# A long convolution beside a gated MLP on one Trainium2 core: the second token tile fetched by transfers of its own, and a new issue order

## The chip, the cores and the metric

The kernel runs on one core of a Trainium2 chip. The time is the device time of one launch in microseconds (us), and less is better. The median of three runs is 256.29 us (256.15 to 256.86).

The engines are named as the profile names them: PE (TensorE, matmuls; PEld is its weight load), DVE (VectorE), ACT (ScalarE), POOL (GpSimd) and SP (SyncE). SP does no arithmetic here. It issues nearly all transfers between DRAM and the on-chip memory, one after another, and so does ACT for a few at the start. Each engine works through its own list of instructions in order.

## What is computed

There are 2048 tokens of 640 channels. With `xn` the layer norm of `A_q`, the result is `A_q` plus a gated long convolution plus a gated MLP (cut to what matters):

```python
def _A_ref(q, k, v, shift_k, ssm_k, ssm_D):
    k_shift = ...            # four taps over time, by channel
    kv = k_shift * v
    y = ...                  # kv convolved with ssm_k over 2048 steps, by FFT of 4096
    y = y + kv * ssm_D
    return q * y
def _B_ref(x, w_gate, w_up, w_down):
    g = x @ w_gate           # 640 -> 1728
    u = x @ w_up
    return (sigmoid(g) * u) @ w_down
xn = _layernorm(A_q)
return A_q + _A_ref(xn, A_k, A_v, A_shift_k, A_ssm_k, A_ssm_D) + _B_ref(xn, B_w_gate, B_w_up, B_w_down)
```

## The kernel before

**Tokens.** The tokens stand in 16 tiles of 128, tile `m` in `acc[:, m, :]`, which holds `A_q` at first and collects both branches. A tile is fetched by quarters of 32 partitions (`load_x`, whose transfer is recorded at profile line L352): quarters 0 and 1 through SP's queue, 2 and 3 through ACT's for tiles 0 to 3, all through SP's for the others. Tiles 0 to 3 make up pass 0, tiles 4 to 7 pass 1, and so on to pass 3.

**The MLP.** For each pass the tokens are normed (statistics L639 to L659, norm L683 on DVE or L685 on ACT) and transposed, on PE for passes 0 and 1 (L705, copied to `xnT` at L314 or L315) and by a transposing transfer through DRAM for passes 2 and 3 (L699). Then 14 chunks of the hidden width follow: five matmuls for the gate and five for the up side (L770, output in `g`), sigmoid on ACT (L735, L729), product on DVE (L737, L732) into `hT`. Pass 0 begins with two chunks in pieces of 128 tokens (L750), so that the first product needs only tile 0. After the chunks, seven matmuls at a time (L786) multiply `hT` with `wd`, and DVE adds the result to `acc` (L798).

Weights are fetched in pieces `w{pass}_{n}`, even `n` for the gate and odd for the up side (`load_w`, L368 to L378). Passes 0 and 1 share one set; passes 2 and 3 load theirs again. Four buffers called `w` hold most pieces, and a further four, `wv`, lie in the buffer `V` until the convolution needs it. A piece that is to go into a buffer in use waits for the buffer's last matmul.

**The convolution.** It runs over ten groups of channels. DVE forms `kv` from `kt` and `vt` (L470 to L488); PE transforms over one factor of the time axis (L508, 32 short matmuls; copied to `T`), then the other (L528, 32 short matmuls each; copied to `S`); DVE multiplies the spectra (L552 to L567), for groups 3 to 9 after two transfers that swap the halves of `S` (L548, `P<-S`); PE transforms back (L580, and L582 for group 0; copied to `V`) and, once for each half of the channels, last L612, 64 short matmuls at a time, whose result is multiplied by the normed tokens (L620) and added to `acc` (L621). The results of L508, L528, L580 and L612 go through three PSUM buffers called `c`, those of L705, L770 and L786 through two called `g`.

**Order.** The function first records every operation with what it reads and writes and on which engine it may run (`plan.op`). An operation is a group of instructions: one transfer, five matmuls, one copy. `ORDER` is a list, written out in full, of the numbers of all operations, which count the calls of `plan.op`. `emit` goes through it and issues each operation on its engine; so it sets the order on each engine, and also which of several buffers an operation gets: an empty one, else the one whose user finished longest ago. Copies that may run on either ACT or DVE run on ACT, unless their number is in `ON_DVE`.

**The start.** Operation 4 is a group of 12 matmuls on zeros, the later seven of the same kind are operation 104 (L816). Operations 5 to 8 fetch tile 0, 10 to 13 tiles 1 to 3 together (120 KB a quarter), 14 and 16 the first halves of the first two weight pieces, operation 9 is a square root on ACT of no further use (L821).

The lines around the end: the result leaves through `store` (L630), four quarters for each range of tiles, the last tile in two halves of 320 columns.

Of the kernel before, what the change touches and what calls it, by code (L numbers as in the profile page):

```python
# [15 lines left out]
ACT = mybir.ActivationFunctionType  # L16
# [26 lines left out]
def _dft_tables():  # L43
# [34 lines left out]


ORDER = [  # L80
    2, 0, 5, 4, 6, 8, 7, 10, 71, 72, 12, 73, 1, 11, 13, 14, 42, 74, 75, 91, 96, 76, 77, 78, 16, 81, 86, 79, 80, 92,
    625, 87, 97, 88, 104, 82, 83, 98, 84, 85, 93, 99, 626, 89, 90, 94, 148, 100, 18, 149, 102, 61, 607, 62, 9, 643,
    608, 63, 101, 150, 103, 19, 639, 645, 153, 641, 43, 627, 629, 152, 640, 642, 635, 67, 637, 628, 630, 17, 609, 611,
    64, 636, 15, 68, 638, 617, 619, 610, 44, 20, 650, 154, 612, 66, 651, 618, 652, 151, 157, 65, 620, 158, 155, 156,
    613, 3, 615, 621, 57, 58, 614, 105, 623, 107, 622, 616, 644, 106, 624, 603, 605, 631, 56, 119, 604, 633, 108, 632,
    606, 115, 599, 116, 634, 646, 601, 600, 648, 109, 647, 111, 122, 60, 59, 602, 112, 661, 113, 649, 673, 662, 665,
    674, 677, 110, 114, 24, 120, 663, 22, 675, 29, 664, 666, 676, 45, 32, 26, 23, 25, 133, 679, 117, 678, 121, 118,
    123, 130, 653, 680, 654, 27, 134, 21, 681, 31, 135, 683, 655, 682, 28, 181, 124, 183, 136, 656, 669, 684, 657,
    658, 670, 30, 33, 672, 34, 126, 35, 667, 163, 659, 668, 660, 162, 165, 127, 685, 671, 164, 125, 716, 36, 167, 166,
    687, 718, 686, 37, 168, 38, 743, 182, 688, 47, 744, 159, 172, 745, 171, 717, 703, 161, 719, 720, 705, 50, 725,  # L90
    727, 169, 39, 170, 704, 160, 51, 706, 726, 173, 128, 178, 698, 728, 729, 174, 180, 700, 707, 131, 175, 699, 709,
    708, 54, 186, 176, 701, 710, 177, 179, 721, 739, 192, 298, 711, 702, 723, 129, 184, 741, 740, 53, 40, 95, 194,
    299, 722, 41, 52, 195, 185, 742, 193, 187, 724, 188, 189, 69, 196, 227, 218, 228, 201, 300, 46, 689, 48, 691, 734,
    690, 49, 190, 199, 736, 233, 202, 692, 197, 200, 301, 234, 198, 55, 217, 191, 693, 137, 304, 730, 735, 216, 737,
    229, 132, 732, 213, 219, 215, 230, 731, 733, 712, 738, 714, 221, 694, 138, 696, 203, 713, 205, 214, 207, 695, 715,
    831, 139, 697, 231, 220, 209, 303, 143, 204, 232, 206, 747, 224, 222, 210, 811, 140, 141, 761, 208, 305, 223, 748,
    211, 762, 751, 225, 235, 237, 236, 833, 226, 263, 212, 764, 772, 254, 264, 755, 265, 144, 269, 302, 252, 253, 267,
    771, 239, 266, 255, 268, 756, 758, 749, 270, 285, 750, 256, 287, 257, 142, 306, 752, 759, 249, 251, 286, 238, 241,
    250, 242, 753, 70, 258, 832, 760, 240, 763, 754, 757, 746, 260, 262, 288, 407, 245, 773, 146, 291, 775, 246, 243,
    765, 244, 271, 272, 786, 788, 247, 766, 261, 273, 410, 275, 767, 318, 248, 274, 259, 768, 320, 769, 319, 277, 278,  # L100
    289, 770, 290, 409, 276, 321, 324, 325, 279, 294, 322, 323, 787, 292, 297, 789, 774, 293, 315, 317, 280, 776, 316,
    782, 307, 784, 326, 281, 783, 790, 282, 308, 310, 327, 838, 283, 785, 839, 309, 284, 777, 311, 840, 295, 340, 354,
    779, 328, 312, 812, 342, 341, 330, 834, 778, 358, 411, 355, 780, 329, 331, 296, 356, 313, 360, 781, 334, 335, 826,
    145, 791, 836, 357, 332, 835, 828, 333, 414, 345, 361, 837, 338, 827, 359, 314, 829, 336, 412, 817, 337, 344, 830,
    822, 362, 343, 351, 819, 339, 824, 823, 352, 818, 363, 792, 346, 825, 347, 408, 353, 793, 404, 427, 348, 364, 349,
    365, 795, 413, 820, 797, 794, 350, 428, 431, 796, 406, 405, 432, 821, 367, 370, 799, 433, 429, 430, 383, 802, 798,
    424, 366, 368, 804, 434, 371, 369, 425, 417, 803, 374, 800, 372, 147, 375, 373, 805, 416, 813, 435, 801, 806, 419,
    384, 418, 421, 420, 422, 385, 454, 808, 807, 815, 426, 386, 809, 387, 376, 814, 377, 436, 415, 463, 464, 378, 379,
    438, 437, 866, 844, 449, 388, 816, 450, 886, 389, 453, 854, 810, 451, 845, 469, 465, 380, 467, 439, 855, 926, 423,
    927, 847, 390, 381, 470, 468, 850, 460, 466, 441, 858, 440, 443, 444, 860, 462, 851, 452, 841, 382, 861, 853, 461,  # L110
    391, 392, 393, 455, 842, 867, 864, 928, 442, 457, 485, 490, 397, 394, 456, 471, 843, 846, 862, 486, 398, 399, 401,
    458, 487, 400, 863, 445, 446, 868, 489, 459, 447, 865, 848, 870, 488, 448, 499, 500, 472, 877, 503, 501, 879, 505,
    849, 504, 474, 878, 476, 506, 473, 475, 502, 491, 496, 479, 498, 480, 477, 478, 497, 852, 493, 507, 492, 494, 856,
    483, 481, 484, 880, 508, 495, 857, 869, 859, 482, 510, 521, 871, 571, 512, 515, 516, 527, 522, 523, 881, 509, 872,
    883, 531, 533, 511, 528, 578, 532, 529, 874, 534, 882, 513, 514, 884, 585, 530, 535, 873, 875, 519, 520, 524, 525,
    536, 876, 929, 931, 885, 517, 930, 887, 518, 901, 526, 592, 932, 549, 888, 903, 538, 906, 550, 551, 553, 537, 539,
    541, 540, 555, 902, 890, 552, 889, 556, 904, 542, 554, 543, 544, 891, 905, 892, 557, 897, 894, 899, 893, 898, 558,
    395, 396, 545, 895, 921, 896, 907, 546, 900, 923, 908, 922, 910, 559, 924, 912, 547, 548, 560, 561, 563, 564, 562,
    565, 913, 566, 569, 567, 915, 909, 568, 570, 579, 911, 925, 580, 914, 933, 582, 917, 572, 916, 934, 581, 583, 935,
    919, 584, 573, 918, 575, 574, 576, 586, 920, 944, 577, 960, 938, 587, 939, 589, 945, 402, 593, 941, 588, 590, 591,  # L120
    966, 962, 594, 947, 936, 963, 596, 942, 937, 943, 595, 961, 597, 965, 598, 940, 946, 403, 970, 969, 948, 950, 949,
    952, 968, 951, 953, 954, 971, 956, 973, 967, 975, 974, 972, 955, 964, 957, 958, 977, 979, 978, 976, 959, 981, 983,
    982, 980
]
ON_DVE = [
    101, 103, 133, 134, 135, 136, 656, 658, 884, 875, 525, 518, 915, 570, 581, 575
]


# [90 lines left out]
def kernel(  # L220
# [100 lines left out]
    def dma(fn, nd, run, q="SP", **kw):  # L321
        few = 1.4 if nd <= 64 and run > 1000 else 1.0
        plan.op({q: (0.48 + nd / 8000.0, lambda: fn(nc.sync if q == "SP" else nc.scalar))},
                size=1.05 * few * nd * (10.6 + run / 23.8) / 16e3 + 0.03, **kw)
# [26 lines left out]
    def load_x(q, m0, m1, eng, pri):  # L351
        dma(lambda e: e.dma_start(acc[32 * q:32 * q + 32, m0:m1, :], xq4[q][:, m0:m1, :]), 32, 1280 * (m1 - m0), q=eng,  # L352
            w=[("acc", m, q) for m in range(m0, m1)], pri=pri)
# [8 lines left out]
    def load_w(tr, n, pri):  # L362
        key, w = weight(tr, n)
        nb = max(0.0, pri - 14)
        kw = dict(pri=pri, nb=nb)
        al = [(key[0], "V")] if key == ("wv", 0) else [] if len(key) == 2 else [(key[0], "w")]
        if n == 6:
            dma(lambda e: e.dma_start(w()[:, :, 0:192], wgr[:, :, 1536:1728]), 640, 384, w=[key + (0,)], alloc=al, **kw)  # L368
            dma(lambda e: e.dma_start(w()[:, :, 256:384], wur[:, :, 1536:1664]), 640, 256, w=[key + (1,)], **kw)
            dma(lambda e: e.dma_start(w()[:, :, 192:256], wur[:, :, 1664:1728]), 640, 128, w=[key + (2,)], **kw)  # L370
            return
        f0, src = 512 * (n // 2), (wgr, wur)[n % 2]
        if tr == 0 and n < 2:
            for h in range(2):
                dma(lambda e, h=h: e.dma_start(w()[:, :, 256 * h:256 * h + 256], src[:, :, f0 + 256 * h:f0 + 256 * h + 256]),
                    640, 512, w=[key + (h,)], alloc=al if h == 0 else (), pri=pri + 0.5 * h)
        else:
            dma(lambda e: e.dma_start(w()[:], src[:, :, f0:f0 + 512]), 640, 1024, w=[key + (0,), key + (1,)], alloc=al, **kw)  # L378
# [425 lines left out]
    FIX = -1e6  # L804
# [14 lines left out]
        load_x(q, 0, 1, "SP", FIX)  # L819
        load_x(q + 2, 0, 1, "ACT", FIX)  # L820
    plan.op({"ACT": (1.35, lambda: nc.scalar.activation(eps2, eps, ACT.Sqrt))}, r=[("eps",)], w=[("eps2",)], pri=FIX + 2)  # L821
    for q in range(2):
        load_x(q, 1, 4, "SP", FIX + 1)
        load_x(q + 2, 1, 4, "ACT", FIX + 1)
    load_w(0, 0, FIX + 2)
    load_w(0, 1, FIX + 2)
    dma(lambda e: e.dma_start(Ft[:], Fdram.ap()), 128, 640, w=[("F",)], pri=11.0, nb=9.0)
# [100 lines left out]
```

## Time and profile before

| | |
|---|---|
| median of three runs | 256.29 us |
| the profiled execution | 259.03 us |
| its span | 257.1 us |
| mean granted clock of PE, as a share | 0.989 |
| moved by transfers | 41.44 MB, mean 161 GB/s |

The span of the profile runs from the first instruction to the last transfer; the profiled execution's own time has some 1.9 us around it, and the executions without a profile are shorter by 2.7 us. In the lines that follow, a timeline line gives the start in us, the duration, the engine (SPq and ACTq are issues of transfers), the source line, the operation with its output and input, and in brackets how long the engine had been idle before it and what ended that. "issue" there means that nothing which the profile shows was waited for. Lines of the windows give a stretch, then its length and for each engine the busy time and the instructions, then the granted clock of PE, the share of the 16 transfer engines that was busy, and GB/s.

### The profile page before, as it was taken

How to read it: one execution, taken by the hardware profiler on the slowest of the kernel's cores; microseconds unless marked ns; L12 is line 12 of the kernel's file. 1: busy time of each engine (PE TensorE's matmuls, PEld its weight loads, DVE VectorE, ACT ScalarE, POOL GpSimd, SP SyncE). 2: the span in 40 equal slices, each digit the busy share in tenths (PEclk: the TensorE clock that was granted, in tenths of full speed). 3: DMA queues.
4: the chain of work that ended last, by engine and by line, in shares of the span. 5: the costliest groups of instructions: out<-in, count | busy, mean ns of one | idle time of the engine just before them, and what ended most of it. 6: DMA issues, size and time to landing. Idle time of an engine off the chain costs nothing.

```text
span 257.1 us, 9461 instructions
## 1 busy us (share of the span) xinstructions
PE 242.6 (94%) x4231; PEld 146.0 (57%) x4231; DVE 201.1 (78%) x337; ACT 175.3 (68%) x259; POOL 0.7 (0%) x6
## 2 busy tenths in 40 slices
PE   8999999999998999999999997699999999798991
PEld 3744446764454567666554544477765554365770
DVE  4613624679999799999999999669999998786731
ACT  3722789577998899787998885655788785452200
POOL 1000000000000000000000000000000000000000
PEclk9999999999999999999999999989999999999998
DMA  6999999999994527999999829953217386002472
GB/s 179 303 289 226 214 304 130 154 143 180 223 261 123 136 87 223 157 135 131 162 185 262 227 44 301 208 128 87 54 32 207 69 273 177 10 3 56 105 188 70
DMA packets 91024, 41.44 MB, mean 161 GB/s; under 512 B 66656, under 2 KB 88104, under 8 KB 90664
## 3 DMA queue, kind: packets, MB, share of 16 engines
q1 hardware_dynamic: 90792, 40.52, 74.3%
q8 instruction: 33, 0.54, 0.9%
q10 hardware_dynamic: 192, 0.33, 0.4%
q14 instruction: 7, 0.06, 0.1%
HBM read 30.61 MB, written 5.24 MB: 139 GB/s over the span
## 4 chain that ended last, share of the span: by engine, by line
PE 79%; DVE 7%; ACT 5%; DMA 4%; issue 3%; ACTq 1%; DVEq 0%
PE g L770 36%; PE g L786 25%; PE c L528 7%; PE c L612 4%; PE c L580 3%; DMA w<-in_B_w_up_dram 2%; PE c L508 2%; ACT S L314 1%; DMA acc<-in_A_q_dram 1%; DVE kvt L488 1%; PE c L750 1%; PE g L705 1%; ACT T L317 1%; DVE hT L737 1%; DVE ta L475 1%
## 5 line engine op out<-in xcount | busy, mean ns | idle before, releaser
L770 PE MATMUL g<-xnT,w 128*128 128x512 bf16 x380 | 90.9, 379 | 1.7 <-DMA w<-in_B_w_up_dram 1.4
L786 PE MATMUL g<-wd,hT 128*128 128x320 bf16 x448 | 67.3, 303 | 2.9 <-issue 2.9
L770 PEld LDWEIGHTS <-w 128*128 128x128 bf16 x380 | 34.9, 98 | 39.8 <-DMA w<-in_B_w_up_dram 1.9
L786 PEld LDWEIGHTS <-hT 128*128 128x128 bf16 x448 | 42.3, 99 | 19.7 <-issue 3.1
L314 ACT CAST S<-c 128x1024 bf16<-128x1024 f32 x40 | 39.6, 1022 | 8.5 <-PE c L528 8.3
L737 DVE TENSOR_TENSOR hT<-sig,g 128x512 bf16<-128x512 bf16 x32 | 21.9, 685 | 17.6 <-PE g L770 17.3
L770 PE MATMUL g<-xnT,V 128*128 128x512 bf16 x140 | 32.6, 379 | 0.0
L735 ACT ACTIVATE sig<-g 128x512 bf16<-128x512 f32 x32 | 19.2, 600 | 15.2 <-PE g L770 13.6
L798 DVE TENSOR_TENSOR acc<-g,acc 128x320 bf16<-128x320 f32 x32 | 15.5, 488 | 17.0 <-PE g L786 16.8
L528 PEld LDWEIGHTS <-Mt 64*128 64x128 f16 x1280 | 20.4, 96 | 9.2 <-issue 8.6
L528 PE MATMUL c<-T,Mt 64*128 64x64 bf16 x1280 | 23.1, 192 | 2.7 <-issue 2.7
L317 ACT ACTIVATE T<-c 128x1024 bf16<-128x1024 f32 x20 | 19.9, 1027 | 5.2 <-PE c L508 5.0
L770 PEld LDWEIGHTS <-V 128*128 128x128 bf16 x140 | 13.4, 98 | 15.4 <-issue 0.4
L488 DVE TENSOR_TENSOR kvt<-ta,vt 128x1024 bf16<-128x1024 bf16 x10 | 21.4, 2142 | 0.1
L314 ACT CAST V<-c 128x1024 bf16<-128x1024 f32 x18 | 18.2, 1025 | 3.2 <-PE c L580 3.1
L314 ACT CAST T<-c 128x1024 bf16<-128x1024 f32 x19 | 18.8, 1023 | 1.6 <-PE c L508 1.6
L729 ACT ACTIVATE sig<-g 128x512 bf16<-128x512 f32 x18 | 10.8, 600 | 5.2 <-PE g L770 4.2
L561 DVE TENSOR_TENSOR S<-S 128x1024 bf16<-128x1024 bf16 x20 | 13.8, 688 | 0.3
L475 DVE TENSOR_TENSOR ta<-ta,tb 128x1024 bf16<-128x1024 bf16 x20 | 13.7, 686 | 0.3
L470 DVE TENSOR_TENSOR tb<-kt,sT 128x1024 bf16<-128x1024 bf16 x20 | 13.8, 688 | 0.1
L567 DVE TENSOR_TENSOR S<-P 64x1024 bf16<-64x1024 bf16 x18 | 12.4, 689 | 0.6
L565 DVE TENSOR_TENSOR S<-S 64x1024 bf16<-64x1024 bf16 x18 | 12.4, 687 | 0.6
(82 smaller groups left out, 240.1 us busy)
## 6 DMA issues: line engine op xcount, KB each, us to landing
w<-in_B_w_gate_dram SPq DMA_DIRECT2D x7, 640.0 KB, 6.5
w<-in_B_w_up_dram SPq DMA_DIRECT2D x7, 640.0 KB, 5.1
P<-S SPq DMA_DIRECT2D x14, 256.0 KB, 3.7
kt<-in_A_k_dram SPq DMA_DIRECT2D x8, 320.0 KB, 6.2
vt<-in_A_v_dram SPq DMA_DIRECT2D x8, 320.0 KB, 6.8
xnd<-xq SPq DMA_DIRECT2D x4, 640.0 KB, 5.4
ht<-in_A_ssm_k_dram SPq DMA_DIRECT2D x16, 96.0 KB, 5.4
wd<-in_B_w_down_dram SPq DMA_DIRECT2D x3, 480.0 KB, 9.6
```

The costliest lines, as they stand in the source:

```text
L314: fa = lambda: nc.scalar.copy(out=out_fn(), in_=in_fn())
L317: fa = lambda: nc.scalar.activation(out_fn(), in_fn(), ACT.Copy, scale=scale)
L470: dve(1024, 2, lambda: nc.vector.tensor_tensor(tl[c][:], sl(tl[kb], 3 - m), sh(m), ALU.mult) if c != o else nc.vector.tensor_tensor(tl[c]. ...
L475: dve(1024, 2, lambda: nc.vector.tensor_tensor(tl[a][:], tl[a][:], tl[c][:] if c != o else tl[c].rearrange("p b n j -> p n b j"), ALU.add) ...
L488: dve(1024, 1 if kt else 2, lambda: nc.vector.tensor_tensor(by_j(tl[o]) if kt else tl[o][:], tl[a].rearrange(form), sl(tl[vb], 0).rearrang ...
L528: nc.tensor.matmul(tl[c][:, b, 64 * kk:64 * kk + 64], lhsT=Mb[rows, k, 64 - 64 * r:192 - 64 * r], rhs=tl[T][rows, 2 * k + r].rearrange("p ...
L561: dve(n, 2, lambda b=b: nc.vector.tensor_tensor(X(b), X(b), H(b), ALU.mult), r=[(Z, b, 0)] + sr, w=[(S_, "p", b)], pri=pri + 0.01)
L735: act(512, lambda: nc.scalar.activation(tl[sg][:], pv(0), ACT.Sigmoid), r=[pk(0)], w=[(sg,)], alloc=[(sg, "sig")], pri=pri - 2000)
L737: dve(512, 1, lambda: nc.vector.tensor_tensor(hT[:, fc, :], tl[sg][:], pv(1), ALU.mult), r=[pk(1), (sg,)], w=[(hk, fc)], pri=pri - 2000)
L770: nc.tensor.matmul(tl[c][:], lhsT=w()[:, k, o:o + P], rhs=tl[X][:, k, :], start=(k == 0), stop=(k == NC - 1))
L786: nc.tensor.matmul(tl[pd[i]][:, 0:320], lhsT=hT[:, fc, t4 * P:(t4 + 1) * P], rhs=wd[:, fc, 320 * i:320 * i + 320], start=(fc == 0), stop=( ...
L798: dve(320, 1, lambda i=i, m=m, pd=pd: nc.vector.tensor_tensor(acc[:, m, 320 * i:320 * i + 320], tl[pd[i]][:, 0:320], acc[:, m, 320 * i:320 ...
```

## The change

The tiles 1 to 3 were fetched by one transfer for each quarter. Now tile 1 has four transfers of its own (operations 10 to 13, 40 KB each) and tiles 2 and 3 four others (14 to 17, 80 KB each). All operations recorded after them have numbers that are higher by four. `ORDER` is replaced as a whole, and `ON_DVE` too.

```diff
-    for q in range(2):
-        load_x(q, 1, 4, "SP", FIX + 1)
-        load_x(q + 2, 1, 4, "ACT", FIX + 1)
+    for m0, m1 in ((1, 2), (2, 4)):
+        for q in range(2):
+            load_x(q, m0, m1, "SP", FIX + 1)
+            load_x(q + 2, m0, m1, "ACT", FIX + 1)
```

```diff
 ORDER = [
-    2, 0, 5, 4, 6, 8, 7, 10, 71, 72, 12, 73, 1, 11, 13, 14, 42, 74, 75, 91, 96, 76, 77, 78, 16, 81, 86, 79, 80, 92,
...
+    6, 2, 0, 4, 5, 46, 7, 8, 16, 17, 75, 76, 67, 15, 14, 12, 13, 11, 77, 1, 78, 79, 90, 95, 85, 86, 87, 10, 18, 88,
...
 ON_DVE = [
-    101, 103, 133, 134, 135, 136, 656, 658, 884, 875, 525, 518, 915, 570, 581, 575
+    103, 105, 139, 140, 662, 38, 530, 586, 600, 593
 ]
```

What the new order does, where the prediction speaks of it:

- Loads at the start. SP: two quarters of tile 0, a quarter of tiles 2 and 3, a quarter of tiles 4 to 7 (160 KB), the other quarter of tiles 2 and 3, two quarters of tile 1, then the first weights. ACT: two of tile 0, two of tiles 2 and 3, two of tile 1.
- DVE's statistics and norms of pass 0 go tile 0, tile 2, tile 1. PE's first operations are the 12 and then the 7 matmuls on zeros, the transposes of tiles 0, 2 and 1, and only then the first L750 group (before: transposes of tile 0, the 7 matmuls, transposes of tile 1, the first L750 group).
- The first L528 group of the convolution stands earlier among PE's operations, with five L770 groups and one L508 group fewer before it.
- Weight pieces of passes 2 and 3 are used in another order and get other buffers. In the last pass `w3_0` and `w3_4` are issued before the first L612 groups of the first half, where it was after them; `w3_5` is still the last piece.
- Copies that moved from DVE to ACT: one of `xnT` of pass 0 and one of pass 1, two norms of pass 1, three of `hT`, one of `T`, two of `V` and two of the last L612 groups. From ACT to DVE: one of `xnT`, one of `kt`, one of `T`, three of the last L612 groups.
- Operation 9 stands at the end of ACT's list, behind the last copy.
- In the last tile the first half of the columns is finished before the second is begun (before: both halves of the sum over the first seven chunks, then both over the rest). One store of tile 14 stands between those of the two halves.

## The prediction

> **What bounds the kernel now.** I read the busy times first, then TensorE's timeline for its gaps, then the chain of waits, then both ends of the span instruction by instruction.
>
> The busy times (engine, us, share, instructions):
>
> ```profile
> PE 242.6 (94%) x4231; PEld 146.0 (57%) x4231; DVE 201.1 (78%) x337; ACT 175.3 (68%) x259; POOL 0.7 (0%) x6
> ```
>
> TensorE (PE) is the bound: no order of the others can save more than its idle time. Its timeline gives the real matmuls from 8.25 to 251.66 us, so idle time inside them is worth looking for. These gaps are all over 0.3 us (start, us, what; idle before it in brackets):
>
> ```profile
> 82.50 0.99 PE L528 MATMUL c<-T,Mt 64*128 64x64 bf16 x56 [1.09 <-issue]
> 160.37 0.51 PE L528 MATMUL c<-T,Mt 64*128 64x64 bf16 x23 [1.62 <-issue]
> 165.39 3.00 PE L786 MATMUL g<-wd,hT 128*128 128x320 bf16 x13 [2.09 <-issue]
> 220.93 2.33 PE L770 MATMUL g<-xnT,w 128*128 128x512 bf16 x10 [1.42 <-DMA w<-in_B_w_up_dram]
> 234.28 2.06 PE L786 MATMUL g<-wd,hT 128*128 128x320 bf16 x14 [0.81 <-issue]
> ```
>
> Three of the four "issue" gaps lie inside one operation, where no data is waited for. PE's instructions come in 33 transfers of 16 KB on the queue called "instruction" (one per 256 instructions), and transfers of it lie at 79 and 83, 158, 162, 231 us, so I read them as late instructions. The gap at 220.93 is another thing. The chain of waits has the piece that ends it, and its last piece of all:
>
> ```profile
> 214.78 6.10 DMA w<-in_B_w_up_dram
> ...
> 251.68 0.49 DVE acc L798
> ```
>
> The last load of weights goes out when PE leaves the buffer that it reuses, and takes 6.10 us. The start, in order of time:
>
> ```profile
> 0.73 1.84 ACTq L352 DMA_DIRECT2D acc<-in_A_q_dram  x4
> 0.73 1.78 SPq L352 DMA_DIRECT2D acc<-in_A_q_dram  x4
> 2.60 1.28 ACT L657 ACT_TABLE_LOAD   x1 [2.60 <-issue]
> 2.70 0.40 SPq L375 DMA_DIRECT2D V<-in_B_w_gate_dram  x1
> 5.99 0.89 DVE L639 BATCH_NORM_STATS2 bs<-acc 128x6 f32<-128x320 bf16 x2 [0.40 <-DMA acc<-in_A_q_dram]
> 8.25 0.45 PE L705 MATMUL g<-ident,xq 128*128 128x128 bf16 x5 [0.27 <-DVE xq L683]
> 8.54 1.28 PE L750 MATMUL c<-xnT,V 128*128 128x128 bf16 x20
> ```
>
> Each queue issues four loads of x at 0.46 us each; the norm of token tile 1 (the second) waits for them, and its transposes (L705) release the first product (L750) at 8.54. From there PE is never idle for more than 0.1 us until 81. The end is SP's:
>
> ```profile
> 235.08 19.93 SPq L630 DMA_DIRECT2D out_dram<-acc  x24
> 254.59 0.42 SPq L630 DMA_DIRECT2D out_dram<-acc  x1
> ```
>
> Looked at closely, the last 14 stores follow each other every 0.463 us from 248.56, so the end is the issue of stores behind the last additions, not PE alone.
>
> **The change, part by part.** Steps of PE are those of the chain of waits: five L770 1.08 us, seven L786 0.95, 32 L528 0.50, 32 L508 0.34, eight L580 0.45, five L705 0.28, twenty L750 1.12.
>
> *Start.* ACT issues six loads instead of four, 2 x 0.46 = 0.92 us more: the table load begins at 3.52 instead of 2.60, ends at 4.80, and the first square root moves from 4.62 to 4.82. SP issues seven before the first weights instead of four, one of them 160 KB for tiles 4 to 7: V goes out at 2.70 + 3 x 0.445 = 4.04 and 4.48 us, and with the medians to landing of these 320 KB loads in the first 60 us (5.5 and 5.2) is there at 9.5 to 9.7. The statistics now take tile 2 first and tile 1 behind it. The quarters of tile 2 are ready about where tiles 1 to 3 were, 5.9: 640 KB lie ahead in both. From there VectorE does, one after another, L639 0.89, L641 0.21, L639 0.49, L659 0.16, L639 0.49, L641 0.21, norm L683 0.45, 0.16, norm of tile 1 0.45: 3.5 us, to 9.5 (before: 8.20). One transpose, 0.28, and L750 starts at 9.8 instead of 8.54. One transpose more is done by then, so the loss is 9.8 - 8.54 - 0.28 = 1.0. The second group of warming matmuls (L816, 1.67) moves ahead of the first transposes and hides in the same wait. Bounds: 40 KB loads land in 1.8 us and 120 KB in 3.5, so 80 KB may be there 0.6 earlier: 0.4; V behind 160 KB more, at the 217 GB/s of the first 10 us, is 0.7 later: 1.7.
>
> *Last weights.* The reused buffer is left earlier: between its last reader and the first reader of the new load stood four L770 groups and one L580 group, 4.8 us, against 6.10 to landing (gap worked out 1.3, seen 1.42). Now seven and two, 8.5 us. The two swap transfers ahead of it on SP wait for four copies of S on ACT; by 0.93 us each these end 1.9 us behind the last L528 group, the issue 1.3 later, the landing 1.3 before use. Gain 1.4; bounds 0 to 1.5.
>
> *Other weights.* Three loads come closer to their use: w2_4 7.1 us (by the same count; 6.6 once two swaps are issued), w2_2 6.2, w3_3 6.0. Nearest rows: 6.1 for the load above, 6.5 as the median of one pair, 7.9 as that of another among busy queues. With 6.5, 6.5 and 6.1 the waits are 0, 0.3 and 0.1: 0.4. Bounds 0 and 1.3 + 1.7 + 1.9 = 4.9. Behind PE's wait ScalarE and VectorE wait with it, no more.
>
> *Convolution earlier among PE's work.* Its first L528 group comes after five L770 groups and an L508 group fewer, 5.7 us of PE work. vt0, on which it hangs, lands where it did (12.2 MB issued up to it in both). Counting VectorE's instructions from the first half's k on (0.61 per product, 2.08 per L488, 0.92 per half of Mt), kvt1 is ready 0.3 us before its use, where 1.2 us was left, and a PSUM slot frees about 0.15 late. I take 0.3; bounds 0 and 1.5.
>
> *Evacuations.* Twelve casts and norms go from VectorE to ScalarE, six the other way: by their rows VectorE 4.4 us less, ScalarE 5.2 more. Costed at nothing: between 60 and 220 us the windows show VectorE busy for 93% and ScalarE for 80%, both under PE's own work. Without that cover one late cast is 1.0 us.
>
> *Square root (op 9).* On ScalarE behind its last copy: 1.28 + 0.19 us, with nothing queued behind it. Nothing; its end near 244 is 12 us before the span's.
>
> *Late instructions.* Unknown, the trace has no after. Their gaps lie where many short matmuls come together. PE time of the densest runs of 256 matmuls by the steps above: before 4.4, 4.6, 5.0, 5.1, 5.5; after 4.2, 4.4, 5.0, 5.0, 5.2. I take no change. Bounds: all gone, 1.09 + 1.62 + 2.09 + 0.81 = 5.6 and 1.4 of slow clock, so -7.0; one more like that at 163, +3.5.
>
> *Tail.* The last tile's first half is now finished before its second is begun, 0.95 us earlier, and one store of the tile before stands between the halves. From the last addition but two: three stores, a pause of 0.5, nine more: last issue at 250.3 + 8 x 0.463 = 254.0 instead of 254.59. Gain 0.6; bounds 0 to 0.9.
>
> Sum: +1.0 - 1.4 + 0.4 + 0.3 + 0 - 0.6 = -0.3 us. The profiled execution is 259.03 us for a span of 257.1; the median of the runs shown is 256.29, 2.7 below it. The terms are differences, so I carry them over: 256.0 us, no change that can be told (a measurement of this kernel can't tell less than about 0.3%, 0.8 us).
>
> **The rivals.**
>
> *Weights land late (slower).* From the point where a load into a just freed buffer takes over 6.2 us while other transfers run, PE waits at each of three places. For it: the row of 7.9 us, and DMA shares of 0.9 and more there. Against it: the load at 214.78 took 6.10 with swaps beside it. At 7.9 for w2_4 and w2_2, and 6.5 for w3_3: 1.3 + 1.7 + 0.5 = 3.5 instead of 0.4: 259.1 us.
>
> *Cold start (slower).* Between 7.8 and 9.8 us PE would do two transposes, 0.56 us. After the gap at 163 (2.30 us with 0.30 busy) the windows show the granted clock at half:
>
> ```profile
> 166.50:168.40 1.90, 1.90 (x12) 0.85 (x11) 0.00 (x0) 0.00 (x0) 0.00 (x0) 0.50 1.03 221
> ```
>
> There thirteen L786 and eighty L528 took 4.4 us instead of 3.0. The same at the start: +1.4, 257.4 us. Against it: the idle time is shorter. The Trainium skill ("TensorE: Matmul & The Clock Gate", Part 1) says that an idle window of about 3.4 us halves the clock; by that the new start would keep its clock and the sum would stay. The trace, where 2.3 us did it behind an earlier gap of 1.6, bears that out only in part.
>
> *Instructions in time (faster).* Two weight loads of the last pass (w3_0, w3_4) go ahead of the dense stage near 155, so the queues are freer when instructions are fetched there. If half of the 7.0 us goes: 252.5 us. Against it: the transposing load still falls there, and a gap at 233 came with idle queues.
>
> *The start is not later.* "Transfers of its own" should let tile 1 start sooner; they are issued last here, which speaks against it. If V and tile 2 land 1 us sooner than I count, the first term is gone: 255.0 us.
>
> **How the numbers follow.** The forecast with its own spread (254.9 to 257.4) 0.41: faster 0.11, same 0.20, slower 0.10. Late weights 0.25, all slower. Cold start 0.09: slower 0.08, same 0.01. Instructions in time 0.20, faster. No later start 0.05: faster 0.04, same 0.01. Together faster 0.35, same 0.22, slower 0.43. The range 252.4 to 259.6 holds the middle of every case and leaves out the far sides of the two large rivals, about 2 in 10.
>
> **What would show it.** L750's first group at 9.8 us, and the last V load landed just ahead of it; no gap that w ends at the last L770 groups; gaps named after a w load at w2_4, w2_2, w3_3 and their size; "issue" gaps adding up to 5 to 6 us; the last store's issue 0.6 us closer to the last L786. I am wrong if the start keeps 8.5, if "issue" gaps add up to under 3 or over 9 us, or if ScalarE's added work shows as PE's releaser.

## The result and the profile after

The changed kernel took 259.26 us (median of four runs, 258.94 to 260.85) against 256.22 us, 1.0107 times as long, with a 95% interval of 1.0062 to 1.0153: slower by 3.0 us by the medians. In two later sets of runs beside the kernel before it was 1.0141 (1.0050 to 1.0232) and 1.0213 (1.0158 to 1.0268). All ratios leave out runs that are over 1.5% above the fastest of the same kernel.

The two profiled executions can't show this by their lengths: 259.03 us before, 258.95 us after. The one before is a long one of its kernel. In twelve later runs of the kernel before, unchanged, the times lay between 255.17 and 258.14 us. So the profiles have to be compared part by part, and against more than one profile of each kernel.

The busy times after, in the same columns:

```profile
PE 242.8 (94%) x4231; PEld 145.8 (57%) x4231; DVE 197.0 (77%) x331; ACT 182.8 (71%) x266; POOL 0.7 (0%) x6
```

PE's work has not changed; VectorE has 4.1 us less and ScalarE 7.5 us more. Now what PE waited for, first before, then after (waiting instruction, what it waited for, us in all, times, longest):

```profile
PE g L786 <- issue: 2.9, 2, 2.1
PE c L528 <- issue: 2.7, 2, 1.6
PE g L770 <- DMA w<-in_B_w_up_dram: 1.4, 1, 1.4
...
PE g L705 <- DVE xq L683: 0.3, 1, 0.3
```

```profile
PE c L612 <- issue: 3.5, 2, 2.7
PE g L770 <- DMA w<-in_B_w_gate_dram: 1.8, 2, 1.4
...
PE g L770 <- DMA w<-in_B_w_up_dram: 0.9, 1, 0.9
PE g L705 <- DVE xq L683: 0.7, 2, 0.5
PE g L770 <- DVE hT L737: 0.5, 1, 0.5
PE g L770 <- ACT sig L735: 0.4, 1, 0.4
PE c L528 <- issue: 0.2, 1, 0.2
```

The late instructions shrank from 5.6 to 3.7 us, and new waits took their place: 1.8 us for gate weights, and more at the start. One profile of each kernel doesn't settle the first of these: later profiles have 4.9 and 2.6 us of late instructions for the order before and 5.7 for the new one. The start, from the timelines of SP and PE:

```profile
0.73 3.86 SPq L352 DMA_DIRECT2D acc<-in_A_q_dram  x7
4.64 0.65 SPq L375 DMA_DIRECT2D V<-in_B_w_gate_dram  x1
5.75 0.38 SPq L375 DMA_DIRECT2D V<-in_B_w_up_dram  x1
```

```profile
9.05 0.45 PE L705 MATMUL g<-ident,xq 128*128 128x128 bf16 x5 [0.45 <-DVE xq L683]
9.75 0.45 PE L705 MATMUL g<-ident,xq 128*128 128x128 bf16 x5 [0.24 <-DVE xq L683]
10.04 0.67 PE L750 MATMUL c<-xnT,V 128*128 128x128 bf16 x9
```

The first product begins at 10.04 instead of 8.54 us, behind VectorE's norms. Then ScalarE's timeline a little later, which holds what the prediction did not look at:

```profile
16.02 0.60 ACT L735 ACTIVATE sig<-g 128x512 bf16<-128x512 f32 x1 [0.48 <-PE g L770]
19.18 0.74 ACT L646 ACTIVATE jk<-acc 128x640 bf16<-128x640 bf16 x1 [2.55 <-DMA acc<-in_A_q_dram]
...
19.91 0.58 ACT L735 ACTIVATE sig<-g 128x512 bf16<-128x512 f32 x1
```

A statistic of tiles 4 to 7 (L646) stands in ScalarE's queue ahead of a sigmoid and waits 2.55 us for x. Before, the first of them came at 27.84 us. The new order wants these tiles 9 us earlier, and SP issues 960 KB of x for tiles 4 to 15 ahead of the fourth piece of V, where it was 320 KB (two more pieces of `w` go ahead of it too). What the transfers moved in the first 20 us, before and then after (the last columns are PE's clock, the share of the transfer engines, GB/s):

```profile
0.00:10.00 10.00, 8.37 (x51) 4.10 (x52) 5.78 (x20) 5.25 (x13) 0.70 (x6) 1.00 0.78 217
10.00:20.00 10.00, 10.00 (x92) 6.35 (x92) 2.85 (x6) 3.17 (x6) 0.00 (x0) 1.00 1.13 290
```

```profile
0.00:10.00 10.00, 8.03 (x34) 3.40 (x35) 5.61 (x19) 4.08 (x9) 0.70 (x6) 1.00 0.70 188
10.00:20.00 10.00, 10.00 (x99) 6.58 (x97) 2.79 (x6) 4.70 (x10) 0.00 (x0) 1.00 1.11 262
```

By 20 us (217 - 188 + 290 - 262) x 10 us = 0.57 MB less has come. By the traces, the fourth piece of V landed at 25.38 us, 0.3 us before its first use at 25.68; in the two profiles of the kernel before it landed at 20.48 and 21.16. The chain of waits after has the late pieces of weights, the late instructions and the end:

```profile
132.41 8.23 DMA w<-in_B_w_gate_dram
...
165.13 2.65 issue
...
217.06 6.05 DMA w<-in_B_w_up_dram
...
252.49 0.49 DVE acc L798
```

From 252.49 to the span's end at 257.2 it is 4.7 us; before it was 5.4.

To compare many executions I worked out PE's lost time from the matmul records: the start of a group, minus the PE work ahead of it by the prediction's steps (and 0.58 us for 64 L612, from the chain of waits). It needs no waits to be named, and it holds slow clock too. Each column is read at the first group that begins when so much work is done; the names of runs are explained below.

```
lost us at work of   18 us   40 us  117 us  140 us  150 us  210 us
before                8.24    8.29   12.20   13.59   19.86   24.93
b_again (unchanged)   7.96    8.01   11.55   14.25   19.02   24.11
after                 9.31    9.88   12.85   15.57   20.52   25.79
a_again2 (unchanged) 10.22   10.79   13.80   15.80   20.93   28.19
b_split               8.32    8.36   11.13   12.58   16.52   21.66
b_xearly             12.53   12.58   15.35   16.75   20.39   25.73
a_start2             11.00   11.57   14.60   16.45   22.01   28.53
a_wfirst             11.72   12.29   15.31   16.87   22.51   26.98
a_xstat2              8.72   10.38   13.37   16.23   21.83   28.44
a_fixed2              8.83   10.49   13.48   14.86   20.29   25.17
```

The first two pairs of rows are the two kernels: the changed one is behind by 1.6 to 2.8 us when 40 us of work are done, and by 0.9 to 4.1 us at 210.

### The profile page after: what moved, and what is told of

It is laid out like the page before. It is cut to its first block, busy times and chain, and to the rows that moved or that the text cites. A ratio compares the mean times of both kernels' runs of the same rounds, so it can differ in the third digit from the quotient of the medians.

```text
span 257.2 us, 9470 instructions
## 1 busy us (share of the span) xinstructions
PE 242.8 (94%) x4231; PEld 145.8 (57%) x4231; DVE 197.0 (77%) x331; ACT 182.8 (71%) x266; POOL 0.7 (0%) x6
## 4 chain that ended last, share of the span: by engine, by line
PE 66%; DMA 14%; DVE 8%; ACT 4%; issue 2%; SPq 2%; ACTq 1%
PE g L770 26%; PE g L786 25%; DMA w<-in_B_w_up_dram 6%; PE c L528 5%; PE c L612 4%; DMA V<-in_B_w_gate_dram 4%; PE c L580 3%; DMA w<-in_B_w_gate_dram 3%; ACT S L314 3%; PE c L508 2%; SPq L352 2%; DMA acc<-in_A_q_dram 1%; DVE ta L475 1%; DVE hT L737 1%; DVE P L558 1%
## 5 line engine op out<-in xcount | busy, mean ns | idle before, releaser
L770 PE MATMUL g<-xnT,w 128*128 128x512 bf16 x380 | 90.1, 380 | 3.4 <-DMA w<-in_B_w_gate_dram 1.8
L786 PE MATMUL g<-wd,hT 128*128 128x320 bf16 x448 | 66.7, 303 | 0.0
L770 PEld LDWEIGHTS <-w 128*128 128x128 bf16 x380 | 34.9, 98 | 42.8 <-DMA w<-in_B_w_gate_dram 2.7
L786 PEld LDWEIGHTS <-hT 128*128 128x128 bf16 x448 | 42.6, 99 | 17.2
L737 DVE TENSOR_TENSOR hT<-sig,g 128x512 bf16<-128x512 bf16 x32 | 21.9, 686 | 18.0 <-PE g L770 14.6
L770 PE MATMUL g<-xnT,V 128*128 128x512 bf16 x140 | 32.7, 379 | 0.4 <-ACT sig L735 0.4
L528 PEld LDWEIGHTS <-Mt 64*128 64x128 f16 x1280 | 19.9, 95 | 6.7 <-issue 5.6
L314 ACT CAST V<-c 128x1024 bf16<-128x1024 f32 x20 | 20.2, 1022 | 3.5 <-PE c L580 3.4
L528 PE MATMUL c<-T,Mt 64*128 64x64 bf16 x1280 | 22.5, 190 | 0.2 <-issue 0.2
L770 PEld LDWEIGHTS <-V 128*128 128x128 bf16 x140 | 13.2, 98 | 15.6 <-issue 0.6
L314 ACT CAST hT<-g 128x512 bf16<-128x512 f32 x18 | 10.8, 600 | 7.5 <-PE g L770 7.5
L612 PE MATMUL c<-V,Bt 32*32 32x80 bf16 x1024 | 10.5, 206 | 3.5 <-issue 3.5
```

Of the source, the lines that this page charges most:

```text
L314: fa = lambda: nc.scalar.copy(out=out_fn(), in_=in_fn())
L528: nc.tensor.matmul(tl[c][:, b, 64 * kk:64 * kk + 64], lhsT=Mb[rows, k, 64 - 64 * r:192 - 64 * r], rhs=tl[T][rows, 2 * k + r].rearrange("p ...
L612: nc.tensor.matmul(tl[cs[g // 2]][32 * q:32 * q + 32, g % 2, 80 * i:80 * i + 80], lhsT=Bb[32 * g:32 * g + 32, n2, r, :], rhs=tl[V][32 * g: ...
L737: dve(512, 1, lambda: nc.vector.tensor_tensor(hT[:, fc, :], tl[sg][:], pv(1), ALU.mult), r=[pk(1), (sg,)], w=[(hk, fc)], pri=pri - 2000)
L770: nc.tensor.matmul(tl[c][:], lhsT=w()[:, k, o:o + P], rhs=tl[X][:, k, :], start=(k == 0), stop=(k == NC - 1))
L786: nc.tensor.matmul(tl[pd[i]][:, 0:320], lhsT=hT[:, fc, t4 * P:(t4 + 1) * P], rhs=wd[:, fc, 320 * i:320 * i + 320], start=(fc == 0), stop=( ...
```

## The experiments

Names that begin with b are edits of the kernel before, with a of the changed one. Ratios are to the kernel before, run beside it on the same chip. The changed kernel itself gave 1.011 to 1.021, so only a ratio outside this band tells an edit of it from it; for the others I go by the profiles.

**The kernel before, again (b_again).** No edit.

> The kernel before, unchanged, profiled again. Theory A (the profile shown was an untypical execution: its late instructions, 5.6 us of gaps called issue and 1.4 us of slow clock, are fewer in most executions): ratio 1.000, the profiled execution near 256.3 us, its gaps called issue 2 to 4 us in all, everything else as before (L750 first at 8.5, one wait of 1.4 us for the last weights). Rival B (being profiled costs this kernel 2.8 us and the changed one nothing): ratio 1.000, the profiled execution near 259 again and the same four gaps of 0.8 to 2.1 us.

Measured: 1.0016 (0.9982 to 1.0051), the profiled execution 257.89 us. Its gaps of late instructions:

```profile
160.83 0.51 PE L528 MATMUL c<-T,Mt 64*128 64x64 bf16 x23 [1.42 <-issue]
166.12 1.94 PE L786 MATMUL g<-wd,hT 128*128 128x320 bf16 x13 [1.22 <-issue]
```

They were 1.62 and 2.09 in the profile before, at the same two instructions. All of them sum to 4.9 us here and to 5.6 there. The next run's profile, in the same order of work and 255.55 us long, has 2.6. So their size moves from execution to execution, and the profile shown had much of it. Rival B is out: the two profiled executions lay 0.9 us above and 1.2 us below the medians of their kernels. Theory A holds in kind, in three profiles of this order of work, but not by its numbers: it had 2 to 4 us of gaps and 256.3 us for this run.

**The split alone (b_split).** The operations of tile 1 in their place, those of tiles 2 and 3 right behind on each queue:

```diff
-SP: 5, 7, 10, 12 (tiles 1-3)     ACT: 6, 8, 11, 13 (tiles 1-3)
+SP: 5, 7, 10, 12, 14, 16         ACT: 6, 8, 11, 13, 15, 17
```

> The order before with the split alone: tile 1 by four transfers of its own where the four of tiles 1 to 3 stood, and the four of tiles 2 and 3 right behind them on each queue. Theory: each queue issues two loads more, 0.9 us, ahead of the first weights, so V lands 0.9 later (9.0 to 9.4 us), past the 8.5 at which L750 began: +0.5 to +0.9, ratio 1.002 to 1.0035. Rival (tile 1 comes sooner, at 4.9 instead of 5.9 us, and V's time does not decide): -0.3 to -0.5 us.

Measured: 1.0011 (0.9972 to 1.0050). The split costs nothing that can be told, and lost time up to 40 us of work (8.36 us) is that of the kernel before (8.29 and 8.01). The split is not the cause. What is left is the new order with its new choice of engines (`ON_DVE`), which no run takes apart.

**The order of the loads in the kernel before (b_xearly).**

```diff
-14, 16, 625, 626, 18, 61, 607, 62, 643, 608, 63, ...
+63, 14, 16, 625, 61, 626, 62, 643, 645, 64, 18, 68, 607, 644, 608, ...
```

(14 and 16 first pieces of V, 607 and 608 third and fourth, 61 to 64 and 68 x; 645 and 644, two pieces of `w`, go ahead of 608 too.)

> The kernel before with the loads of the first 20 us in the changed kernel's order on SP: a quarter of x for tiles 4 to 7 ahead of the first weights, the three others and a quarter of tiles 8 to 15 ahead of V's third and fourth pieces; nothing else moved. Theory (that order of loads makes V's pieces late, by 2 to 3 us): PE waits for V or w at 10 to 30 us, idle time up to 40 us of work 9.0 to 11 us instead of 8.0 to 8.4, ratio 1.004 to 1.011. Rival (the pieces land in time in any order, the loss belongs to ScalarE's queue alone): ratio 0.998 to 1.003.

Measured: 1.0111 (1.0051 to 1.0170). PE's waits and the place:

```profile
PE g L770 <- DMA V<-in_B_w_gate_dram: 3.4, 1, 3.4
```

```profile
22.53 1.25 PE L770 MATMUL g<-xnT,V 128*128 128x512 bf16 x5 [3.38 <-DMA V<-in_B_w_gate_dram]
```

The loads' order alone costs the kernel before as much as the whole change did. The idle time came out above the range given.

**x behind V in the changed kernel (a_xlate).** Five loads (65 to 68 and 72) moved behind 612, the fourth piece of V.

> The changed order with the loads of x for tiles 4 to 15 that stood ahead of the third and fourth weight pieces of V (five loads, 960 KB) moved behind the fourth. Theory (what varies most between executions of the changed kernel is PE's wait for these pieces and for w at 15 to 35 us, 0.5 to 3 us, because x stands ahead of them on SP): PE's idle time up to 40 us of work falls from 9.9 to 12.3 us to 9.2 to 9.8 us, and the time by 0.8 to 2 us: ratio 1.005 to 1.011. Rival (the waits come from the slower start of all transfers, or ScalarE's statistics of tiles 4 to 7 now wait for x and hold up the sigmoids queued behind them): ratio 1.013 to 1.020.

Measured: 1.0457 (1.0393 to 1.0520). The rival's second half happened, in ScalarE's timeline:

```profile
24.24 0.74 ACT L646 ACTIVATE jk<-acc 128x640 bf16<-128x640 bf16 x1 [8.12 <-DMA acc<-in_A_q_dram]
...
24.97 0.58 ACT L735 ACTIVATE sig<-g 128x512 bf16<-128x512 f32 x1
```

The statistic waits 8.12 us, and PE 5.5 us for the sigmoid behind it. So moving the loads back costs more, as long as ScalarE's statistics stand early.

**Both moved (a_xstat, a_xstat2).** The statistics of tiles 4 to 7 (109 to 117) behind the sigmoids too; first in a bunch, then one by one:

```diff
-... 110, 645, 655, 111, 109, 161, 652, 619, 112, 113, 116, 627, 115, 117, 114, 615, 121, 120, 623, ...
+... 645, 655, 161, 652, 110, 619, 111, 627, 109, 615, 112, 623, 113, 116, 605, 115, 609, 117, 641, 114, ...
```

> As the run with x behind V's pieces, and with ScalarE's statistics of tiles 4 to 7 (nine L646, L649 and L652 operations) moved behind the sigmoids that stood behind them, to about where the kernel before had them in the products of pass 0. Theory (the changed kernel loses 1.6 to 4 us in the first 40 us because these statistics stand early on ScalarE, want x for tiles 4 to 7 early, and so put 640 KB ahead of V's third and fourth pieces): the wait of 5.5 us for a sigmoid goes, no wait for V's pieces comes back, PE's idle time up to 40 us of work is 8.9 to 9.6 us instead of 9.9 to 12.3, ratio 1.002 to 1.008. Rival (the start loses because the transfers begin later and nothing behind them matters): idle time 10 us or more, ratio 1.011 to 1.018.

Measured: 1.0381 (1.0307 to 1.0456). Up to 18 us of work lost time was 8.68 us, as the theory has it. Then PE waited 5.4 us for a gate (L737): VectorE's root of tiles 4 to 7 had moved along, stood ahead of it, and waited 5.0 us for the last statistic.

> As the run with x and ScalarE's statistics moved, but with the statistics spread one by one between the sigmoids, three of tiles 8 to 15 moved behind them, and VectorE's square root of tiles 4 to 7 left where the changed kernel has it, so that no product's sigmoid or gate stands behind a bunch of them. Theory (loads and statistics of tiles 4 to 7 are the whole loss at the start): no wait over 1 us in the first 50 us, PE's idle time up to 40 us of work 8.7 to 9.8 us instead of 9.9 to 12.3, ratio 1.004 to 1.012, below the 1.021 of the changed kernel in the call before. Rival (ScalarE has no room for these statistics before the end of pass 0 in this order of products): another wait of 2 us or more for a sigmoid or a gate, ratio 1.015 or more.

Measured: 1.0186 (1.0120 to 1.0251). Lost time at 18 us of work is 8.72 us, against 9.31 to 11.72 in the runs whose loads and statistics were those of the changed kernel; then 1.25 us went to a late copy at 50 us, and weights were waited for by 4.0 us in all, against 2.7 in the changed kernel's profile. The fourth piece of V landed at 20.22 us, as early as in the kernel before, although the pieces of `w` still stood ahead of it. From the first product to 49 us no wait over 0.25 us is left; a_again2, and a_start2 and a_wfirst below, have 0.9 to 1.8 us of waits there for pieces of V and `w`. So the profiles show the cause of the early loss: x ahead of the first weights, for statistics that wait for it. The ratio does not show it: 1.0186 lies among those of the changed kernel and above the 1.004 to 1.012 of the theory.

**Tile 1 ahead of tile 2 (a_start2).** Loads, statistics and transposes of tile 1 first, the first pieces of V ahead of the 160 KB.

> The changed order with the split kept, but tile 1 loaded and normed ahead of tile 2 and the first weights issued ahead of the 160 KB for tiles 4 to 7; nothing else moved. Theory (the start costs the changed kernel 1.3 to 1.5 us, and PE keeps what it gains there, as the curve of idle time in the two traces keeps it up to 120 us): L750 first at 8.6 to 9.3 instead of 10.04, 0.8 to 1.5 us less than the changed kernel. Rival (the transfers in the first 35 us are the limit, all queues being busy, and PE waits for w pieces at 20 to 35 us instead): the same as the changed kernel within 0.4.

Measured: 1.0167 (1.0104 to 1.0229): the rival. L750 began at 8.35, lost time behind it was 8.62 us instead of 9.00 to 9.20, and then PE waited 1.55 us, until 27.36. The profile puts this wait down to a statistic on ScalarE (L652), which ended at the same time; the trace has V's fourth piece landing at 27.31.

**The start of before on the new order (a_start).** The first 58 operations of before, then the rest of the changed order.

> The changed order with the first 58 operations of the order before, the split undone, and the rest of the changed order behind them. Theory (the start costs what the two traces show, L750 at 10.04 instead of 8.54 us with one transpose more done): -1.2 to -1.5 us from the changed kernel, 257.8 to 258.1, ratio to before 1.006 to 1.0075. Rival (PE runs into the same waits a little later, and the time saved at the start is waited for behind it): 259.0 to 259.3, ratio 1.011.

Measured: 1.0390 (1.0326 to 1.0454). L750 began at 8.26, and then PE waited 4.09 us at 22 us for `w`: the new order of products needs other pieces first. This edit tells of neither theory.

**Weights ahead of their swaps (a_wfirst).** Loads 815 (`w2_4`) and 911 (`w3_5`) each ahead of the two swaps before them.

```diff
-330, ..., 331, ..., 815        561, 562, ..., 911
+815, 330, ..., 331, ...        911, 561, 562, ...
```

> The changed order with the loads w2_4 and w3_5 each moved ahead of the two swap transfers that stood before them on SP. Theory (SP's order makes the weights late: w2_4 issued 1.9 us and w3_5 3.3 us behind the last reader of their buffer): the waits of 1.41 and 0.91 us go, w2_2's 0.35 shrinks or stays: -2.0 to -2.6 us, 256.7 to 257.3, ratio 1.002 to 1.004. Rival (the loads take as long in landing when they start sooner, since the queues are full, or the swaps become late and L580 waits for them): 258.5 to 259.3, ratio 1.009 to 1.011.

Measured: 1.0185 (1.0132 to 1.0238). All three waits went: between 117 and 120 us of work the lost time grows by 0.2 us, where it grew by 1.7. But this execution had lost 12.29 us at 40 us of work already (1.1 us of it at 28 us, again for V's fourth piece, landed at 28.03), and the total shows no gain.

**Instruction blocks moved (b_shift, b_shift_bad).** A block is 128 matmuls with their weight loads, the 256 instructions that come in one transfer (see the last section). Same order; only the number of warming matmuls differs:

```diff
-    plan.op({"PE": (4.4, lambda: warm(12))}, ...
+    plan.op({"PE": (4.4, lambda: warm(8, 120))}, ...   # b_shift_bad: warm(8, 32)
```

> The kernel before with its order unchanged; of the first twelve warming matmuls eight are left and 120 very short ones (32x32 by 80) follow, 116 matmuls more in all. So every block of 128 matmuls (256 instructions, one fetch) begins 12 matmuls later in the work. Theory (every gap called issue stands at a block's first matmul, number 128k+86 to 93, because the block before it took less PE time than a fetch needs; PE time of the shortest blocks is 2.2 and 2.3 us in the order before, and 3.0 with the blocks moved): the gaps at 158, 163 and 232 us shrink from 3 to 5.5 us in all to under 1.5: -2 to -3.5 us, ratio 0.987 to 0.993. Rival (the gaps come with the dense work or the busy queues, wherever the blocks begin): the same gaps at the same places in the work, ratio 1.000 to 1.004.

> As the run before, with 32 short matmuls instead of 120: 28 matmuls more than the kernel before, so that the blocks begin 28 matmuls earlier in the work, and the shortest hold 1.5 us of PE time. Theory (blocks): gaps called issue grow to 6 to 9 us in all, +2 to +4 us, ratio 1.008 to 1.016. Rival (dense work or busy queues): ratio 0.999 to 1.003.

Measured: 0.9918 (0.9874 to 0.9963) and 1.0254 (1.0187 to 1.0320). Both went the theory's way, the bad one further. PE's waits in the second:

```profile
PE c L612 <- issue: 4.9, 3, 2.0
PE c L508 <- issue: 1.9, 1, 1.9
...
PE g L770 <- issue: 0.7, 4, 0.2
PE g L786 <- issue: 0.5, 1, 0.5
```

The four of 0.2 us are no late blocks: at each, the trace lacks one matmul's record. The others add up to 7.2 us, within the 6 to 9 of the theory. In b_shift's profile (257.21 us, long for it) 3.3 us remained at block starts, with one gap of 2.2 us at 161 us. So "under 1.5" was too good, and where b_shift gains its time no profile shows. Both profiles also have a wait for a sigmoid at 35 us (1.6 and 0.8 us) that the kernel before doesn't have; its cause is open.

**The block at 165 us (a_dense).** L786 groups moved ahead of the L612 pair (381, 382) and ahead of the L508 group (453):

```diff
-852, 381, 382, ..., 853, ..., 867, 453, ..., 860, ..., 846, ..., 464
+852, 867, 853, 381, 382, ..., 860, 846, 453, ..., 464
```

> The changed order with two L786 groups of seven matmuls moved ahead of the pair of L612 groups at 165 us and two more ahead of the L508 group behind it, and nothing else on PE. Theory (the gap at matmul 2392 is an instruction block that came too late, since the block before it held 2.6 us of PE time; it holds 4.5 to 5.0 now): the gap of 2.65 us shrinks to under 0.8 and the slow clock behind it goes: -1.5 to -3 us, ratio 1.002 to 1.007. Rival (the fetch is late because the transfer queues are busy there, so the gap stays within 0.5 us of its size or moves to the next block): ratio 1.011 to 1.016.

Measured: 1.0162 (1.0107 to 1.0217). The waits:

```profile
PE c L612 <- issue: 1.7, 2, 0.9
...
PE c L508 <- ACT T L317: 1.1, 1, 1.1
PE c L508 <- issue: 0.9, 1, 0.9
```

The gap shrank from 2.65 to 0.9, and 2.0 us came back at the L508 group a little later, half of it for ScalarE's copy of T and half as the next late block. The rival's last words, that the gap moves to the next block, were right.

**All together.** a_all had everything above but the moved statistics.

> All repairs of the changed order together: tile 1 ahead of tile 2, x for tiles 4 to 15 behind the pieces of V, w2_4 and w3_5 ahead of their swaps, and the groups of the run before moved. Theory (the three causes, start, weights behind swaps and the block at 165 us, make up the whole loss, and they are independent): -4 to -6 us from the changed kernel, ratio 0.993 to 1.000. Rival (they overlap, PE's time gained in one place is waited for in the next): ratio 1.005 to 1.012.

Measured: 1.0326 (1.0281 to 1.0370), with a_xlate's wait in it (4.8 us for a sigmoid). a_fixed is a_xstat with tile 1 first and the weights ahead, and has its wait of 5.4 us too: 1.0394 (1.0338 to 1.0450). a_fixed2 is the same on a_xstat2.

> The run with x and the statistics moved, with tile 1 ahead of tile 2 and the loads w2_4 and w3_5 ahead of their swaps as well. Theory: the start and the late weights are the whole loss: another 1.5 to 2.5 us less, ratio 0.995 to 1.001. Rival (what is gained there is lost at the block of instructions at 165 us and at the chain on ScalarE behind it): ratio 1.002 to 1.008.

> The run before with tile 1 ahead of tile 2 and the loads w2_4 and w3_5 ahead of their swaps as well. Theory: 1.5 to 2.5 us less than that run, since the waits of 1.0 to 1.4 us at 130 us and of 0.9 to 1.1 us at 222 us go: ratio 0.997 to 1.005. Rival (the time is waited for behind these places): within 0.8 us of that run.

Measured: 1.0150 (1.0088 to 1.0212) beside a_xstat2's 1.0186. Its profiled execution, 258.45 us, was the shortest of six, and no wait for a weight is left:

```profile
PE c L612 <- issue: 2.9, 2, 1.8
...
PE g L786 <- ACT xnT L314: 1.2, 1, 1.2
PE c L528 <- issue: 1.0, 1, 1.0
```

The ratios of these two can't be told apart. What its other executions, 259.9 to 262.6 us, wait for is open.

**The changed kernel, again (a_again, a_again2).** The ratios stand at the head of the result; the second, 1.0213, is above the range given.

> The changed kernel, unchanged, again beside the kernel before. Theory (its gap called issue of 2.65 us at 165 us and the late weights come with its order, in every execution): ratio 1.008 to 1.015, the profile has a gap of 2.3 to 3.0 us behind matmul 2392 and waits of 1 to 2 us for the weights at 130 to 141 us. Rival (the first four executions were untypical): ratio under 1.006.

> The changed kernel once more, so that the three runs beside it have it on the same chip in the same hour: ratio 1.010 to 1.018; the profile has PE's idle time up to 40 us of work at 9.8 to 12.3 us and the gap of 2.6 to 3.1 us at matmul 2392.

In the profile of a_again2 the gaps of late instructions were

```profile
168.09 0.74 PE L612 MATMUL c<-V,Bt 32*32 32x80 bf16 x70 [2.38 <-issue]
...
187.67 0.34 PE L580 MATMUL c<-At,S 128*128 128x128 f16 x3 [1.64 <-issue]
```

the first at the same instruction as in the changed kernel's first profile, the second new. With three smaller ones they sum to 5.7 us.

**A version ahead of both (b_best).** b_shift with the changed kernel's tail.

> The kernel before with its instruction blocks moved as in the run with 120 short matmuls, and the tail of the changed kernel (the last tile's first half finished and stored before its second half is begun). Theory (the tail gives 0.6 to 0.7 us, as the two traces show it: 4.7 instead of 5.4 us from the last addition to the end): ratio 0.986 to 0.992. Rival (the tail's gain is lost, as the stores' landing sets the end): ratio 0.991 to 0.994.

Measured: 0.9939 (0.9902 to 0.9975). With b_shift it is the one that beats both kernels. The ratio lies in the rival's range; the tail's 0.7 us can't be told in it.

## Why the prediction failed

It forecast no change, from -0.3 us, and the kernel became 3.0 us slower. Three terms of its sum failed: the start, the last weights and the other weights. It took them as 1.0 - 1.4 + 0.4 = 0, and the profiles show some 1.6 to 2.8, -0.5 and +1.8, together 2.9 to 4.1 us. With the tail's -0.7 it is 2.2 to 3.4, about what was measured. By the prediction's own chances, slower (0.43) was more likely than no change (0.22); it gave the late weights 0.25, and nothing to a start that goes on. The measured 259.26 us lies inside its range, which ends at 259.6, but the range reaches so far because of the rival of late weights.

Against the two profiles themselves the sum was nearly right: -0.3 us forecast, +0.1 us seen in the span. That is luck. The profiled execution of the kernel before was 2.7 us over its median and had much of the late instructions (5.6 us, against 4.9 and 2.6 in two others of its order), while the changed kernel's had little of them (3.7, against 5.7 in a_again2). So this pair differs by -1.9 us in a term that varies between executions by more than that, and this hid the three terms above. Setting its change to 0 was not what failed.

- **Start, +1.0, right up to the first product and cut short there.** L750 was forecast at 9.8; it came at 10.04, and at 9.84 in a_again2. But the loss goes on: at 40 us of work the changed kernel is behind by 1.6 to 2.8 us, up to 1.1 over the bound of 1.7. The prediction counted 160 KB of x ahead of the first weights; ahead of V's fourth piece 960 KB stood instead of 320, and ScalarE's statistics that need them had moved ahead of sigmoids. b_xearly shows that such an order of loads costs the kernel before as much, a_xlate that the loads alone can't be put back, and a_xstat2 that with both moved the early loss shrinks to 8.7 us at 18 us of work (before: 8.2).
- **Last weights, -1.4, seen -0.5** (a wait of 0.91 instead of 1.42). The prediction let the two swaps ahead of the load wait for ScalarE's four copies of S. These had ended by 212.9. The swaps went out at 215.71, right behind VectorE's last product of the spectra (L567), which ended at 215.65. SP's own waits between 210 and 218 us:

```profile
SPq L548 <- DVE S L567: 3.7, 1, 3.7
```

The load followed at 217.06 and took 6.05, so it landed 0.9 us behind its use and not 1.3 ahead of it.
- **Other weights, +0.4, seen +1.8.** `w2_4` cost 1.41 and `w2_2` 0.35 in this profile. The gap of 7.1 us was counted right; SP spent 2.27 us on two swaps ahead of `w2_4`, not the half a microsecond taken off. a_wfirst, where they stand behind the load, has no wait there, so these were the cause. `w3_3` cost nothing. The rival of late weights named this, and its 259.1 us is near the result, but only 1.8 of its 3.5 us are there.
- **Convolution +0.3 and evacuations 0.** PE's rows show 0.36 us for a sigmoid and 0.46 us for a gate, neither at the convolution. The sigmoid is ScalarE as PE's releaser, the last of the prediction's three signs of being wrong.
- **Late instructions, 0, seen -1.9 in the two profiles**, but +0.8 from b_again to a_again2. The measure was wrong: runs of 256 matmuls anywhere. A block is 128 matmuls with their weight loads, at fixed places; see below.
- **Tail, -0.6, seen -0.7.**
- **Cold start** did not happen: the clock is 1.00 in the first 20 us of the windows.

What stays open is the whole size. Its three ratios lie between 1.011 and 1.021, and no repair brought the changed kernel back. In a_xlate, a_xstat, a_start and a_dense another wait of 1 to 5.5 us stood behind the one that was taken away. In a_wfirst and a_fixed2 the waits for late weights did go, and the ratio stayed where it was. So the account rests on the waits and the lost time in the profiles, and no total confirms it. What the moved copies (`ON_DVE`) do by themselves was not tried.

## What to carry to other kernels

When an order is searched anew, list for each queue what now stands ahead of the first things that the bound engine needs, on the computing engines as well as on SP: here statistics that had moved forward came with their input, and V's fourth piece landed at 25.4 instead of 20.5 us. Take more than one profile before adding terms to a base, and ask which term makes the profiled execution longer than its median. Late instructions are a matter of place: count the work in each block, and try moving the blocks.

## What the hardware showed

Late instructions have fixed places. Counting matmul records from the start, the gaps called issue stand at these numbers:

```
before    733   2265   2392   3927
b_again   733   2265   2392   2776   3927
after     2264   2392   3926
a_again2  2264   2392   2774   2902   3926
```

All differ by multiples of 128, to within 4 (an instruction now and then is neither a matmul nor a weight load). The 4231 matmuls and their weight loads are 8462 instructions, and 33 transfers of 16 KB came on the queue "instruction", one for 256 of them. In the profiles without missing records, PE went on 1.2 to 1.6 us after the end of such a transfer at each of these gaps (in the changed kernel: begun at 165.22, took 1.13, PE on at 167.78). From the first matmul of a block to the first of the next it took 3.4 to 6.9 us wherever there was such a gap; the blocks before these gaps held 2.0 to 5.1 us of PE work. Between these, the transfer begins late by an amount that changes from run to run: for the block at 2392, 2.6 to 4.3 us after the block before it was entered.

The Trainium skill ("Runtime: NRT & Kernel Launch", Instruction fetch mechanics) says that instructions come in blocks of 256, the next fetched while the current one runs. The trace agrees: 33 transfers for 8462 instructions, and the one for the block at 2392 begins 2.6 to 4.3 us after the block before was entered. The same section of the Trainium skill says that the fetch is hidden because instructions are issued more slowly than it fills; here it was not, by 2.6 to 7.2 us an execution, and 28 or 116 more short matmuls at the start made the kernel before slower (1.0254) or faster (0.9918).
